# Identity matmuls while the first keys load, and the first four heads cast and split two by two

## The chip, the core and the metric

The kernel runs on one core of a Trainium2 chip. Its time is the device time of one execution in microseconds, taken as the median of several runs. The engines named below are PE (TensorE matmul) with PEld (its weight loads), DVE (VectorE), ACT (ScalarE), POOL (GpSimd) and SP (SyncE), which here only issues transfers. Each engine works through its own instructions in order, and semaphores hold an instruction back until the work it needs is done.

## What is computed

Sliding-window attention with sink keys (2 batches, 8 heads, 768 positions, head dimension 64) feeds a capacity-limited expert layer, and that feeds a gated layer:

```python
scores = q @ k.T / 8, kept where key < n_sink or 0 <= row - key < window
x = softmax(scores) @ v                      # (1536, 512)
logits = x @ w_gate                          # each token gets one of 8 experts, 192 tokens each
out[mask_e] = relu(x[mask_e] @ w1[e]) @ w2[e]
return ((out @ w_a) * (out @ w_b)) @ w_out
```

## The kernel before

The program has three stages. The attention works on 12 blocks of 128 rows (2 batches, 6 each); then comes the choice of experts; then the expert and gated layers, all in one instruction stream per engine that is written in the order in which it runs.

A block's keys and queries come as one tile `kq` (`load`, line L220), two transfers per block, one for each half of the 128 partitions. For blocks 0 and 1 each of the two is cut again, so that heads 0 to 3 and heads 4 to 7 arrive separately: four transfers of 256 KB per block. All of them stand in SP's queue, in order, and a transfer has to wait for the one that stands eight transfers ahead to have landed, because eight semaphores serve them in turn.

`split_half` prepares four heads of block 0 or 1: ACT casts the keys into `KH` (L243) and the queries into `q` (L244), DVE writes the rest of the keys into `KL` (L245) and the rest of the queries into the lower half of `q` (L246). Later blocks are split by `split` on DVE (L256, L258) and POOL (L257, L259).

`run` then goes through groups of four heads, 24 in all. `scores` does for each head two matmuls into the PSUM tile `sp` (L282, L283), a masked copy with its minimum on DVE (L284), and the exponential on ACT (L286). `turn` transposes with the identity (L300), `values` multiplies by V (L326), `rows` transposes back and multiplies by the gate weights into the PSUM tile `x` (L341). ACT's order in the first round is: casts of heads 0 to 3, two exponentials, casts of heads 4 to 7.

The PSUM pool gives each tile name a fixed number of buffers. `x` has one buffer. Each call of `pp.tile(..., name="x", bufs=1)` makes a new tile on that buffer, which may be written only when the work on the tile before is over. The identity `ident` is made on POOL at the very start. Before the change the first matmul of the program is that of the first scores.

Of the kernel before, what the change touches and what calls it, by code (L numbers as in the profile page):

```python
# [8 lines left out]
F32 = mybir.dt.float32  # L9
# [10 lines left out]
B, H, S, D = 2, 8, 768, 64  # L20
# [12 lines left out]
KC = [0, 128, 256, 416, 544, 704]  # L33
# [18 lines left out]
def kq_start(b, j):  # L52

    return (b * KTOT + KC[j] + 128 * (NJ * b + j)) * D * H


def dram_ap(src, offset, ap):
    return bass.AP(tensor=src.tensor, offset=src.offset + offset, ap=ap)
# [83 lines left out]
class Attention:  # L142
# [70 lines left out]
    def load(self, i):  # L213
        nc, at = self.nc, self.at
        b, j = self.blocks[i]
        w = KW[j]
        r = self.raws[i] = at.tile([128, H, 288], F32, name="kq", bufs=3)
        for h0, h1 in ((0, 4), (4, H)) if i < 2 else ((0, H),):
            for half in range(2):
                nc.sync.dma_start(r[64 * half:64 * half + 64, h0:h1, :w + 128],  # L220
                                  dram_ap(self.kq, kq_start(b, j) + h0 * (w + 128),
                                          [[H * (w + 128), 64], [w + 128, h1 - h0], [1, w + 128]]))
# [10 lines left out]
                nc.sync.dma_start(v[32 * r:32 * r + 32, :, r // 2, 64 * (r % 2):64 * (r % 2) + 64],  # L233
                                  dram_ap(self.vS, (b * 128 + 32 * r) * 2 * D, [[2 * D, 32], [D, 2], [1, D]]))

    def split_half(self, i, half, copy, eng):

        nc = self.nc
        if half == 0:
            self.Q[i] = self.at.tile([128, H, 128], F32R, name="q", bufs=3)  # L240
        hs, c = slice(4 * half, 4 * half + 4), KC[i]
        r, q, kh, kl = (t[:, hs] for t in (self.raws[i], self.Q[i], self.KH[:, :, c:c + 128], self.KL[:, :, c:c + 128]))
        copy(kh, r[:, :, :128])  # L243
        copy(q, r[:, :, 128:256])  # L244
        eng.tensor_tensor(kl, r[:, :, :128], kh.bitcast(F32), op=OP.subtract)  # L245
        return lambda: nc.vector.tensor_tensor(q[64:], r[64:, :, 128:256], q[64:].bitcast(F32), op=OP.subtract)  # L246
# [14 lines left out]
    def run(self, extra):  # L261

        nc, at, pp, ident = self.nc, self.at, self.pp, self.ident
# [7 lines left out]
        def scores(g):  # L271
            i, q = divmod(g, 2)
            b, j = blocks[i]
            c0, w, co, cp, cs = kwin(j)
            if q == 0:
                MN[i] = at.tile([128, H], F32, name="mn", bufs=3)
                SM[i] = at.tile([128, H], F32, name="sm", bufs=4)
            p = P[g] = at.tile([128, 4, 288], F32, name="p", bufs=3)
            out = []
            for h in range(4 * q, 4 * q + 4):  # L280
                sp = pp.tile([128, 288], F32, name="sp", bufs=3)
                nc.tensor.matmul(sp[:, :w], Q[i][:, h], KH[:, h, c0:c0 + w], start=True, stop=False)  # L282
                nc.tensor.matmul(sp[:, :w], Q[i][:, h], KL[:, h, c0:c0 + w], start=False, stop=True)  # L283
                nc.vector.tensor_tensor_reduce(p[:, h % 4, :w], sp[:, :w], self.mask(j), -0.125, 1e30, op0=OP.add,  # L284
                                               op1=OP.min, accum_out=MN[i][:, h:h + 1])
                out.append(lambda h=h: nc.scalar.activation(p[:, h % 4, :w], p[:, h % 4, :w], AF.Exp, bias=MN[i][:, h:h + 1],  # L286
                                                            scale=-1.0, accum_out=SM[i][:, h:h + 1]))
            return out

        def turn(g):  # L290
            i, q = divmod(g, 2)
            c0, w, co, cp, cs = kwin(blocks[i][1])
            p = P[g]
            nsl = 2 if cp is None else 4
            out = []
            for e in range(2):
                tp = pp.tile([128, 4, 128], F32, name="tp", bufs=2)
                for t in range(nsl):
                    c = co if t < 2 else cp
                    nc.tensor.transpose(tp[:, t], p[:, 2 * e + t % 2, c:c + 128], ident)  # L300
                t = T[g, e] = at.tile([128, 4, 128], F32, name="t", bufs=5)
                out.append(lambda t=t, tp=tp: nc.scalar.activation(t[:, :nsl], tp[:, :nsl], AF.Copy))
            return out

        def turn_sink(g):
            i, q = divmod(g, 2)
            cs = kwin(blocks[i][1])[4]
            if cs is not None:
                sp = pp.tile([128, 128], F32, name="ts", bufs=1)
                for h in range(4):  # L310
                    nc.tensor.matmul(sp[NS * h:NS * h + NS], P[g][:, h, cs:cs + NS], ident, start=True, stop=True, skip_group_check=True)
                ST[g] = at.tile([128, 128], F32, name="st", bufs=3)
                nc.vector.tensor_copy(ST[g], sp)
# [20 lines left out]
        def rows(g):  # L334

            i, q = divmod(g, 2)
            x = X[g] = (pp.tile([128, 288], F32, name="sp", bufs=3).rearrange("p (a n) -> p a n", a=2) if g == ng - 1
                        else pp.tile([128, 2, 144], F32, name="x", bufs=1))
            os = OS.pop(g)
            for a in range(2):  # L340
                nc.tensor.matmul(x[:, a], os[:, a], self.ig[:, 2 * q + a].rearrange("p c d -> p (c d)"), start=True, stop=True)  # L341

        def out_rows(g):
            i, q = divmod(g, 2)
            x = X.pop(g)
            hs = slice(4 * q, 4 * q + 4)
            if q == 0:
                XR[i] = self.pre.tile([128, H, D + E], F32, name="xr", bufs=2)
                r = RS[i] = self.pre.tile([128, 2, H], F32, name="rs", bufs=2)
                nc.scalar.activation(r[:, 0], SM[i], AF.Identity, bias=tiny)  # L350
                nc.vector.reciprocal(r[:, 1], r[:, 0])
            nc.vector.tensor_tensor(XR[i][:, hs], x.rearrange("p a (c d) -> p (a c) d", c=2),
                                    RS[i][:, 1, hs][:, :, None].to_broadcast([128, 4, D + E]), op=OP.mult)
            if q == 1:
                nc.vector.tensor_reduce(self.L[:, i], XR[i][:, :, D:].rearrange("p h e -> p e h"), op=OP.add, axis=AX.X)
                nc.sync.dma_start(self.xd[128 * i:128 * i + 128].rearrange("p (h d) -> p h d", h=H), XR[i][:, :, :D])
# [1 line left out]
        self.load(1)  # L358
        self.load(2)
        self.load_v(0)  # L360
        self.split_half(0, 0, nc.scalar.copy, nc.vector)()
        for it in range(-1, ng + 2):
            if it % 2 and (it + 1) // 2 < nb:
                i = (it + 1) // 2
                if i + 1 < nb:
                    self.load_v(i + 1)
                if i + 3 < nb:
                    self.load(i + 3)
            exps = scores(it + 1) if it + 1 < ng else []
            if 0 <= it - 3:  # L370
                out_rows(it - 3)
            for e in exps[:2]:
                e()
            if it == -1:
                self.split_half(0, 1, nc.scalar.copy, nc.vector)()
            elif it == 0:
                self.second()
                for half in range(2):
                    self.split_half(1, half, nc.scalar.copy, nc.vector)()
            elif it == 1:  # L380
                self.others()
                self.split(2, nc.gpsimd)
            elif it % 2 == 0 and it // 2 + 2 < nb:
                self.split(it // 2 + 2, nc.gpsimd)
            ts = turn(it) if 0 <= it < ng else []
            for e in ts[:1]:
                e()
            for e in exps[2:]:
                e()
            for e in ts[1:]:  # L390
                e()
            if 0 <= it < ng:
                turn_sink(it)
            if 0 <= it - 1 < ng:
                copy = values(it - 1)
            if 0 <= it - 2 < ng:
                rows(it - 2)
            if 0 <= it - 1 < ng:
                copy()
            if it == 20:  # L400
                self.wide()
            if it in extra:
                extra[it]()
# [697 lines left out]
```

## Time and profile before

| | |
|---|---|
| median of 3 runs | 641.16 us (639.24 to 641.59) |
| profiled execution | 640.13 us, span 638.3 us |
| PE busy | 582.6 us, 91% of the span |
| DVE, ACT, POOL busy | 361.5, 250.4, 102.4 us |
| mean granted TensorE clock | 0.965 of full speed |
| attention / choice / experts | to about 127 us / to about 166 us / to the end |

The profiled execution is about 1.0 us below the median of the runs. The span is counted from the first to the last instruction and is what the rows below give times in; some 1.8 us lie around it. In the rows, a timeline line gives start, duration, engine, line of the kernel, operation, tiles and shapes, how many were merged (x), and in brackets how long the engine stood idle ahead of it and what ended that. A matmul of plain 32-bit floats appears as two records, each with a weight load of its own; the scores' matmuls and the transposes of L300 appear as one.

### The profile page before, as it was taken

The numbers are of one execution on the slowest core, as the hardware profiler recorded it, in microseconds if no ns is written. First come the engines' busy times: TensorE is split into PE (matmuls) and PEld (weight loads), VectorE is DVE, ScalarE is ACT, GpSimd is POOL, SyncE is SP. The second block draws the span as 40 slices with busy tenths as digits, with TensorE's granted clock in tenths as the row PEclk, the third lists the DMA queues.
The fourth block names the chain that finished last, engine by engine and source line by source line (L and its number), as shares of the span: only waits on it lengthen the run. The fifth ranks groups of instructions, "written<-read, shape, count | busy, mean of one in ns | idle before, by whom it ended". The sixth has DMA issues, their size and how long they took to land.

```text
span 638.3 us, 10373 instructions
## 1 busy us (share of the span) xinstructions
PE 582.6 (91%) x3804; PEld 542.7 (85%) x3804; DVE 361.5 (57%) x913; ACT 250.4 (39%) x655; POOL 102.4 (16%) x150
## 2 busy tenths in 40 slices
PE   3899989922699999999999999999999999999996
PEld 2688868711599999999999999999999999998885
DVE  5776786687336766666633655565557456622330
ACT  4677777600245554554422322322233222322330
POOL 2567765122401010000000000000000000012021
PEclk9999999955699999999999999999999999999998
DMA  9998594420477878767600222222222222102010
GB/s 181 224 205 180 113 265 150 132 83 2 124 235 225 252 233 273 251 197 264 216 16 0 67 67 68 98 67 70 92 71 75 79 79 66 34 17 82 2 67 33
DMA packets 49804, 79.04 MB, mean 124 GB/s; under 512 B 16944, under 2 KB 25168, under 8 KB 49232
## 3 DMA queue, kind: packets, MB, share of 16 engines
q1 hardware_dynamic: 47616, 71.97, 40.4%
q0 software_dynamic: 1984, 6.31, 3.3%
q8 instruction: 32, 0.52, 0.4%
q14 instruction: 28, 0.23, 0.1%
q10 hardware_dynamic: 144, 0.00, 0.0%
HBM read 71.98 MB, written 6.29 MB: 123 GB/s over the span
## 4 chain that ended last, share of the span: by engine, by line
PE 64%; issue 7%; POOL 1%; DVE 0%; ACT 0%; POOLq 0%
PE b L851 13%; PE b L906 10%; PE b L904 10%; PE b L905 10%; PE b L865 8%; PE b L866 4%; PE b L928 3%; PE b L927 3%; PE b L926 3%; POOL out L944 1%; PE b L841 1%; PE b L956 1%; DVE ys L875 0%; ACT y L877 0%; POOLq L1097 0%
## 5 line engine op out<-in xcount | busy, mean ns | idle before, releaser
L906 PE MATMUL b<-y,ml 128*128 128x384 f32 x384 | 128.6, 335 | 0.0
L904 PE MATMUL b<-y,mh 128*128 128x384 f32 x384 | 128.6, 335 | 0.0
L905 PE MATMUL b<-y,mh 128*128 128x384 f32 x384 | 128.5, 335 | 0.0
L851 PE MATMUL b<-xm,wr 128*128 128x192 f32 x512 | 89.1, 327 | 0.1
L851 PEld LDWEIGHTS b<-xm,wr 128*128 128x128 f32 x512 | 82.4, 190 | 0.3 <-issue 0.3
L865 PE MATMUL b<-hh,wh 128*128 128x384 f32 x256 | 79.5, 374 | 0.0
L904 PEld LDWEIGHTS b<-y,mh 128*128 128x128 f32 x384 | 72.1, 188 | 1.1
L905 PEld LDWEIGHTS b<-y,mh 128*128 128x128 f32 x384 | 72.1, 188 | 1.0
L906 PEld LDWEIGHTS b<-y,ml 128*128 128x128 f32 x384 | 72.1, 188 | 0.0
L761 DVE TENSOR_TENSOR wl<-wr,wh 128x512 fp32r<-128x512 f32 x60 | 41.5, 691 | 41.8 <-ACT wh L755 39.3
L944 POOL DMA_INDIRECT out<-xg,idx x6 | 6.2, 1040 | 361.9 <-ACT xg L942 361.1
L866 PE MATMUL b<-hh,wl 128*128 128x192 f32 x256 | 64.1, 250 | 0.0
L286 ACT ACTIVATE p<-p,mn 128x288 f32<-128x288 f32 (+2 forms) x96 | 47.8, 500 | 27.0 <-DVE mn L284 27.0
L282 PE MATMUL sp<-KH,q 128*128 128x288 f32 (+2 forms) x96 | 33.2, 360 | 18.2 <-DVE q L246 12.3
L866 PEld LDWEIGHTS b<-hh,wl 128*128 128x128 f32 x256 | 48.9, 191 | 0.0
L284 DVE CUSTOM_DVE_ANT_0 p<-sp,mk 128x288 f32<-128x288 f32 (+2 forms) x96 | 35.8, 420 | 22.2 <-PE sp L283 21.2
L865 PEld LDWEIGHTS b<-hh,wh 128*128 128x128 f32 x256 | 48.1, 188 | 0.0
L282 PEld LDWEIGHTS sp<-KH,q 128*128 128x128 f32 x96 | 20.1, 209 | 24.2 <-DVE q L246 12.9
L755 ACT ACTIVATE wh<-wr 128x512 fp32r<-128x512 f32 x64 | 39.9, 624 | 0.4 <-DMA wr<-in_w 0.4
L853 ACT ACTIVATE hh<-b 128x192 fp32r<-128x192 f32 x64 | 20.9, 327 | 46.2 <-PE b L851 45.4
L915 ACT ACTIVATE zz<-z 128x384 fp32r<-128x384 f32 x24 | 12.6, 525 | 58.8 <-DVE z L910 58.8
L257 POOL TENSOR_TENSOR KL<-kq,KH 128x1024 fp32r<-128x1024 f32 (+1 forms) x10 | 29.0, 2896 | 40.0 <-DVE KH L256 39.2
(245 smaller groups left out, 1038.3 us busy)
## 6 DMA issues: line engine op xcount, KB each, us to landing
wr<-in_w SPq DMA_DIRECT2D x128, 256.0 KB, 4.2
mr<-in_wm SPq DMA_DIRECT2D x36, 512.0 KB, 3.7
kq<-in_kq SPq DMA_DIRECT2D x12, 512.0 KB, 7.4
kq<-in_kq SPq DMA_DIRECT2D x8, 576.0 KB, 9.8
v<-in_vN SPq DMA_DIRECT2D x12, 256.0 KB, 8.6
xd<-xr SPq DMA_DIRECT2D x12, 256.0 KB, 4.4
kq<-in_kq SPq DMA_DIRECT2D x8, 256.0 KB, 5.3
xg<-xd,idx POOLq DMA_INDIRECT x12, 3.6
```

The costliest lines, as they stand in the source:

```text
L257: eng.tensor_tensor(kl, kr, kh.bitcast(F32), op=OP.subtract)
L282: nc.tensor.matmul(sp[:, :w], Q[i][:, h], KH[:, h, c0:c0 + w], start=True, stop=False)
L284: nc.vector.tensor_tensor_reduce(p[:, h % 4, :w], sp[:, :w], self.mask(j), -0.125, 1e30, op0=OP.add, op1=OP.min, accum_out=MN[i][:, h:h + 1])
L286: out.append(lambda h=h: nc.scalar.activation(p[:, h % 4, :w], p[:, h % 4, :w], AF.Exp, bias=MN[i][:, h:h + 1], scale=-1.0, accum_out=SM[i ...
L755: self.nc.scalar.activation(self.W[u][0], self.R[u, 1], AF.Copy)
L761: (eng or self.nc.vector).tensor_tensor(lo, self.R.pop((u, 1)), hi.bitcast(F32), op=OP.subtract)
L851: nc.tensor.matmul(ps, w[:, 128 * k:128 * k + 128], x[:, k], start=k == 0, stop=k == 3)
L865: nc.tensor.matmul(ps, hi[:, 128 * d:128 * d + 128], hh, start=f == 0, stop=False, skip_group_check=True)
L866: nc.tensor.matmul(ps[:, 0], lo[:, 128 * d:128 * d + 128], hh[:, 0], start=False, stop=f == 7, skip_group_check=True)
L904: nc.tensor.matmul(p, hi[:, w, c], y[:, k, 0], start=k == 0, stop=False)
L905: nc.tensor.matmul(p, hi[:, w, c], y[:, k, 1], start=False, stop=False)
L906: nc.tensor.matmul(p, lo[:, w, c], y[:, k, 0], start=False, stop=k == 3)
```

## The change

Two edits. Sixteen matmuls of the identity with itself go ahead of the first split, each into a newly made tile `x`. And the first four heads of block 0 come in transfers of two heads, and are cast and split two heads at a time; `split_half` becomes `split_some` with the heads given as a range, and does the same work for every later group.

```diff
-        for h0, h1 in ((0, 4), (4, H)) if i < 2 else ((0, H),):
+        for h0, h1 in ((0, 2), (2, 4), (4, H)) if i == 0 else ((0, 4), (4, H)) if i == 1 else ((0, H),):
             for half in range(2):
                 nc.sync.dma_start(r[64 * half:64 * half + 64, h0:h1, :w + 128],
...
-    def split_half(self, i, half, copy, eng):
+    def split_some(self, i, h0, h1, copy, eng):
...
-        hs, c = slice(4 * half, 4 * half + 4), KC[i]
+        hs, c = slice(h0, h1), KC[i]
...
-        self.split_half(0, 0, nc.scalar.copy, nc.vector)()
+
+        for k in range(16):
+            nc.tensor.matmul(pp.tile([128, 2, 144], F32, name="x", bufs=1)[:, 0, :128], ident, ident, start=True, stop=True)
+        self.split_some(0, 0, 2, nc.scalar.copy, nc.vector)()
+        self.split_some(0, 2, 4, nc.scalar.copy, nc.vector)()
...
-                self.split_half(0, 1, nc.scalar.copy, nc.vector)()
+                self.split_some(0, 4, 8, nc.scalar.copy, nc.vector)()
...
-                    self.split_half(1, half, nc.scalar.copy, nc.vector)()
+                    self.split_some(1, 4 * half, 4 * half + 4, nc.scalar.copy, nc.vector)()
```

How PE's instructions stand at the start of the program, with the semaphores each waits for. Before, the scores of the first group come first (`DVE_49` counts finished DVE work):

```order
L282 MATMUL sp<-KH,q 128x128 [waits DVE_49]
L283 MATMUL sp<-KL,q 128x128
L282 MATMUL sp<-KH,q 128x128
L283 MATMUL sp<-KL,q 128x128
L282 MATMUL sp<-KH,q 128x128
L283 MATMUL sp<-KL,q 128x128
```

And PE at the same place with the change (`Pool_49` counts POOL's work, here the identity; `PE_49` counts PE's own finished matmuls):

```order
L363 MATMUL x<-ident 128x128 [waits Pool_49]
L363 MATMUL x<-ident 128x128 [waits PE_49] x15
L282 MATMUL sp<-KH,q 128x128 [waits DVE_49]
L283 MATMUL sp<-KL,q 128x128
L282 MATMUL sp<-KH,q 128x128
L283 MATMUL sp<-KL,q 128x128
L282 MATMUL sp<-KH,q 128x128 [waits DVE_49]
L283 MATMUL sp<-KL,q 128x128
```

The sixteen stand ahead of every other matmul, and fifteen of them wait for PE's own count, which the one before each raises when it is done; the third head's scores now have a wait of their own.

ACT at the start of the program, as a difference (casts of block 0, exponentials of the first group, casts of heads 4 to 7):

```order
-L243 CAST KH<-kq 128x4x128
-L244 CAST q<-kq 128x512
+L243 CAST KH<-kq 128x2x128
+L244 CAST q<-kq 128x256
+L243 CAST KH<-kq 128x2x128
+L244 CAST q<-kq 128x256
 L286 ACTIVATE p,sm<-p,mn 128x128 x2
 L243 CAST KH<-kq 128x4x128
```

Two casts became four of half the size; the casts of heads 4 to 7 still stand behind the first two exponentials. DVE's L245 and L246 change in the same way. SP issues four transfers of 128 KB in place of the first two of 256 KB:

```order
-L220 DMA kq<-in_kq 64x4x256 x8
+L220 DMA kq<-in_kq 64x2x256 x4
+L220 DMA kq<-in_kq 64x4x256 x6
 L220 DMA kq<-in_kq 64x2304 x2
 L228 DMA v<-in_vN 128x512 x2
```

The bytes and their order by heads are the same; the queue is two transfers longer.

## Rows read from the trace of the kernel before

**Rows 1.** The page: span.

```profile
span 638.3 us, 10373 instructions
```

**Rows 2.** The chain that ended last, its earliest work.

```profile
166.37 3.75 PE b L956 x8
```

**Rows 3.** Stretches: busy us of PE, PEld, DVE, ACT, POOL; granted clock, DMA share, GB/s.

```profile
4.00:8.00 4.00, 0.00 (x0) 0.00 (x0) 2.54 (x10) 1.14 (x2) 1.43 (x4) 1.00 1.13 217
8.00:12.00 4.00, 1.97 (x8) 1.78 (x8) 2.58 (x11) 2.35 (x9) 0.00 (x0) 1.00 1.13 203
...
24.00:27.00 3.00, 3.00 (x18) 2.34 (x17) 0.94 (x3) 2.45 (x9) 2.92 (x2) 1.00 1.17 253
```

**Rows 4.** Timeline, the first 11 us.

```profile
1.04 0.29 POOL masks.py:199 TENSOR_SCALAR_AFFINE_SELECT ident<-ident 128x128 f32<-128x128 f32 x1
...
5.71 0.23 DVE L170 TENSOR_SCALAR mk<-mk 128x128 f32<-128x128 f32 x1
6.47 0.62 ACT L243 CAST KH<-kq 128x512 fp32r<-128x512 f32 x1 [4.22 <-DMA kq<-in_kq]
...
7.84 0.69 DVE L246 TENSOR_TENSOR q<-kq,q 64x512 fp32r<-64x512 f32 x1
8.59 0.29 PEld L282 LDWEIGHTS sp<-KH,q 128*128 128x128 f32 x1 [8.59 <-DVE q L246]
...
8.86 0.42 PE L283 MATMUL sp<-KL,q 128*128 128x128 f32 x1
...
9.07 0.41 PE L282 MATMUL sp<-KH,q 128*128 128x128 f32 x1
...
9.31 0.29 DVE L284 CUSTOM_DVE_ANT_0 p<-sp,mk 128x128 f32<-128x128 f32 x1 [0.78 <-PE sp L283]
...
10.48 0.60 ACT L243 CAST KH<-kq 128x512 fp32r<-128x512 f32 x1
```

**Rows 5.** Timeline: lone 32-bit matmuls at 157 and 126 us, and who reads them.

```profile
126.74 0.76 PE L341 MATMUL sp<-ig,os 128*128 128x144 f32 x4
127.53 0.46 DVE L352 TENSOR_TENSOR xr<-sp,rs 128x288 f32<-128x288 f32 x1 [0.19 <-PE sp L341]
...
157.56 0.50 PEld L576 LDWEIGHTS ps<-dc,on 128*128 128x128 f32 x2
...
158.19 0.17 DVE L581 TENSOR_SCALAR bad<-ps 128x8 f32<-128x8 f32 x1 [0.18 <-PE ps L576]
```

**Rows 6.** Timeline of PE: score matmuls at 22 and at 33 us.

```profile
22.25 0.41 PE L282 MATMUL sp<-KH,q 128*128 128x256 f32 x1
22.47 0.41 PE L283 MATMUL sp<-KL,q 128*128 128x256 f32 x1
...
33.28 0.29 PE L282 MATMUL sp<-KH,q 128*128 128x288 f32 x1
33.41 0.30 PE L283 MATMUL sp<-KL,q 128*128 128x288 f32 x1
```

**Rows 7.** Stretches during and after the eight matmuls of L956.

```profile
169.00:170.00 1.00, 1.00 (x4) 0.63 (x3) 0.67 (x1) 0.30 (x1) 0.00 (x0) 0.50 0.20 33
170.00:171.00 1.00, 1.00 (x9) 1.00 (x7) 0.64 (x1) 0.39 (x2) 0.00 (x0) 0.76 0.63 225
```

**Rows 8.** Tile kq: the second and third transfer (durations of issue, then times to landing).

```profile
L220 SPq DMA_DIRECT2D kq<-in_kq x2: 613/615/617, 1.6 to 2.2; - x2
...
DMA to landing us min/median/max: 4.8/5.1/5.3
```

**Rows 9.** Timeline, blocks 2 and 3 being split.

```profile
25.80 2.35 POOL L259 TENSOR_TENSOR q<-kq,q 64x1024 fp32r<-64x1024 f32 x1
26.49 2.20 DVE L256 CAST KH<-kq 128x1024 fp32r<-128x1024 f32 x1 [1.88 <-DMA kq<-in_kq]
28.20 0.40 PE L282 MATMUL sp<-KH,q 128*128 128x288 f32 x1 [0.48 <-POOL q L259]
...
29.55 0.44 DVE L284 CUSTOM_DVE_ANT_0 p<-sp,mk 128x288 f32<-128x288 f32 x1
```

More of the change, by code (lines that the diff above doesn't have):

```diff
@@ L234, in load_v @@
                                   dram_ap(self.vS, (b * 128 + 32 * r) * 2 * D, [[2 * D, 32], [D, 2], [1, D]]))
-    def split_half(self, i, half, copy, eng):
+    def split_some(self, i, h0, h1, copy, eng):
         nc = self.nc
-        if half == 0:
+        if h0 == 0:
             self.Q[i] = self.at.tile([128, H, 128], F32R, name="q", bufs=3)
-        hs, c = slice(4 * half, 4 * half + 4), KC[i]
+        hs, c = slice(h0, h1), KC[i]
         r, q, kh, kl = (t[:, hs] for t in (self.raws[i], self.Q[i], self.KH[:, :, c:c + 128], self.KL[:, :, c:c + 128]))
```

## The prediction

> **What bounds the kernel now.** The page first: the span is 638.3 us [rows 1], and 640.13 us are the profiled execution's time. The chain of waits comes next, but it reaches back only to 166.37 us, the eight matmuls ahead of the experts [rows 2]. The edits act in the first 15 us, so the question is whether a shift there comes out at the end. For that I read the stretches and then the timeline of the start. Up to 8 us PE has nothing to do [rows 3]: the first keys are on their way. The timeline shows the opening chain: ACT waits for the transfer until 6.47, casts, DVE ends the last subtraction at 7.84 + 0.69 = 8.53, PE begins the first scores at 8.59, DVE reads them at 9.31, and ACT, after two exponentials, casts heads 4 to 7 from 10.48 [rows 4]. Everything after hangs on that chain, since ACT and DVE work in order: the later casts stand behind these exponentials.
>
> Is there slack further on that would swallow a shift? The one transfer that DVE waits for later is block 3's, for 1.88 us, until 26.49. But the cast it starts takes 2.20 us, while POOL works on block 2 until 25.80 + 2.35 = 28.15; the next scores start at 28.20, on POOL's heels [rows 9]. So that wait hides behind the POOL chain, which began with the first scores. I take a shift at 9 us as one at the end, less at most the 29.55 - (28.20 + 0.5) = 0.85 us by which DVE's reading of those scores (some 0.5 us after PE's start) is late because of that cast.
>
> **The change part by part.** *Halved transfers.* The second transfer lands at 1.6 + 4.8 = 6.4 us, the third at 2.2 + 5.3 = 7.5 to 7.6 [rows 8], so 256 KB take about 1.2 us in the queue and the first lands at about 5.2 (estimate). Two transfers of 128 KB for heads 0 and 1 are the same 256 KB: about 5.2 instead of 6.4, and heads 2 and 3 at 6.4. Issuing takes SP about 0.6 us each [rows 8]; two more cost 1.2 us of SP, whose transfers queue for longer than that, so the later blocks' bytes do not come later. Price 0; if the small transfers starve the engines at the start, up to +0.6 us on heads 4 to 7, which are not needed before 10.48.
>
> *Halved casts and subtractions.* ACT's cast of 512 columns takes 0.62 us, DVE's subtraction 0.69 [rows 4]; halves cost between half and the whole of that, I take 0.4 each. DVE is busy with the mask until 5.71 + 0.23 = 5.94 [rows 4]. Heads 0 and 1: ACT from 5.25 on, DVE at about 5.95 to 6.75. Heads 2 and 3: ACT from 6.45, DVE about 6.9 to 7.7. So the first scores could begin at 6.8 instead of 8.59, and DVE, whose subtractions for heads 2 and 3 stand ahead of the first reading, could read at about 7.75 instead of 9.31: a gain of about 1.5 us, if PE were free.
>
> *Sixteen matmuls.* The identity is ready at 1.04 + 0.29 = 1.33 [rows 4], so PE starts at about 1.4. Each of the other fifteen waits until PE's count says that the one before it is done, which the order shows; so what counts is the whole time of a lone matmul, weight load to count, not the step of a stream. No row shows such a wait on the matmul just before. The nearest rows: the first score pair is two 128-column passes, each with its weight load, just as one identity matmul is two records; from the first load at 8.59 to the end of the second pass at 8.86 + 0.42 = 9.28 it takes 0.69 us, and DVE starts 0.03 later [rows 4]. A lone 32-bit matmul of 8 columns takes from 157.56 to DVE's 158.19, 0.63 us [rows 5], and 120 columns more in each of two passes can add up to 0.2. PE in turn starts 8.59 - 8.53 = 0.06 after DVE ended [rows 4]. So a step is 0.69 + 0.05 = 0.74 us, at most 0.85, at the slow clock. The bottom end is the fast clock: two matmuls of four records at 126.74 end 0.03 before DVE's 127.53, so 0.76 us for both; the second adds two passes of about 0.12, which leaves 0.5 for one and 0.55 with the wait.
>
> Which clock? The column of granted clock reads 1.00 from the start, but nothing ran on PE before 8.59, and the starts say otherwise: 256 columns 0.22 us apart at 22.25, 288 columns 0.13 apart at 33.28 [rows 6], that is the 1.2 and the 2.4 GHz level. Between lies a stretch in which PE was busy without a break (24 to 27) [rows 3]. At 166.37 eight matmuls stream back to back for 3.75 us [rows 2], and the granted clock goes from 0.50 to 1.00 just after them, in the microsecond from 170 [rows 7]. Scores with gaps between (1.97 us busy of 4 at 8 to 12) [rows 3] did not raise it, though those go on for 12 us. Sixteen matmuls that each wait for the last leave the array idle for much of each step (two loads and two passes of about 0.11 in 0.74), so they resemble the second case; I take the slow level throughout.
>
> Then the sixteen end at 1.4 + 16 x 0.74 = 13.2, and the first scores, whose operands have been ready since 6.8, start at about 13.1 instead of 8.59 (a load may begin a little ahead of the end before it). Queued behind them on PE are all scores; DVE's reading waits for these, ACT's exponentials for DVE, and the casts of heads 4 to 7 stand behind those. **Sum: +4.5 us** on the profiled execution, 640.13 + 4.5 = 644.6. That execution is 1.0 us under the median of the runs, 641.16, from which the same sum gives 645.7. I predict 645.2. The bounds: steps of 0.85 us end at 15.0, +6.4, thus 646.5 to 647.6; the 0.85 us of slack make the least 643.8.
>
> The Trainium skill, TensorE: Matmul & The Clock Gate, section Single matmul latency, gives (219 + N)/1.2 ns for one matmul at the slow clock, 289 ns for 128 columns. Taken for the whole step with one more pass it would be about 0.4 us by that page (an estimate), sixteen would end near 7.7 us, and nothing would be delayed. The rows say 0.69 for the two passes with their loads.
>
> **The rivals.** *A: the sixteen raise the clock.* For it: PE would be occupied from 1.4 on without a long gap. Against it: the gaps inside each step, and that later bursts of scores did not do it. If the level rose halfway, eight steps of 0.74 and eight of 0.55 end at 1.4 + 5.9 + 4.4 = 11.7, +3.1 on the first scores; had it been high from the start, 10.2, +1.6. The fast level then gives back, up to 27 us: a pair of score matmuls takes 0.43 at the slow level (8.86 less 0.21 to 9.07, twice [rows 4]) and half at the fast one, 0.6 us over three pairs of a group and 0.2 on the first pair's latency; 0.8 for each of about four groups, 3.2 at most, less where DVE or ACT is the slower. Net between -1.6 and +0.6: 639.5 to 641.8 on the median, middle 641. The same page's table at the end advises to warm up with matmuls ahead of the work that matters; by it this rival is the case, and only the waits between the matmuls speak against it.
>
> *B: the waits cost next to nothing, PE overlaps the matmuls.* This ends on the other side. The step would be that of the score stream, 0.21 us [rows 4], the sixteen end at 4.8, and the halved casts give their 1.5 us: 639.7 on the median, and 636.5 if the clock were up as well. It decides as soon as the step is below (6.8 - 1.4)/16 = 0.34 us. Against it stand the lone pair's 0.69 and the wait in the order.
>
> *C: the shift is swallowed*, by transfers that wait less or by DVE getting its casts of block 3 in earlier. For it: the 1.88 us wait [rows 9]. Against it: POOL's chain ends behind it. It would leave at most 4.5 - 1.9 = 2.6: 643.8.
>
> **How the numbers follow.** The forecast has 0.62, A 0.18, B 0.10, C 0.10. Half a per cent, about what a measurement of this kernel can tell from no change, is 3.2 us. In the forecast the time is above 644.4 in about 0.55 of the 0.62 (the rest is a step near 0.69 with some slack); A adds 0.01 above and 0.03 below 638, B 0.05 below, C 0.02 above. Faster 0.08, same 0.34, slower 0.58. The range from 639.0 to 648.0 takes in the forecast with its bounds, C and nearly all of A, and leaves out half of B and clocks that rise late; the likeliest case's own range is 643.5 to 647.8.
>
> **What would show it.** In the profile of the changed kernel: sixteen groups of two L363 records from about 1.4 us, 0.7 to 0.8 us apart (0.55 would be A, 0.21 B), PE's first L282 at about 13 with nothing but PE ahead of it, ACT's first cast at about 5.3, DVE's last subtraction of the four heads at about 7.7, then DVE idle until about 13.8 on L283. The casts of heads 4 to 7 come at about 15.0, and PE's start of block 2 at about 32.7 instead of 28.20. The start of the experts' matmuls at 166.37 moves to about 170.8; if it moves by clearly less than the first scores, something took up the shift that I did not see. The forecast is wrong if 256-column scores already step by 0.11 us before 20 us, or if the sixteen are over by 8 us.

## The result, and the profile after

The changed kernel takes 647.07 us (median of 6 runs, 646.05 to 648.13), the kernel before in the same comparison 641.12 us (6 runs, 639.24 to 641.59). The ratio is 1.0089, with a 95% interval of 1.0072 to 1.0107: slower by 0.9%, 5.95 us. (A ratio, here and below, is an estimate of its own beside the medians and need not be their quotient.) The profiled execution takes 646.05 us, 5.92 more than that of before.

The start of the timeline of the kernel after (columns as in [rows 4]; the lines of the code have moved by up to 4):

```profile
1.38 0.50 PEld L363 LDWEIGHTS x<-ident 128*128 128x128 f32 x2 [1.38 <-POOL ident masks.py:199]
1.38 13.60 PE L363 MATMUL x<-ident 128*128 128x128 f32 x32 [1.38 <-POOL ident masks.py:199]
...
2.23 0.50 PEld L363 LDWEIGHTS x<-ident 128*128 128x128 f32 x2 [0.35 <-PE x L363]
...
5.23 0.41 ACT L243 CAST KH<-kq 128x256 fp32r<-128x256 f32 x1 [2.98 <-DMA kq<-in_kq]
...
6.35 0.40 ACT L243 CAST KH<-kq 128x256 fp32r<-128x256 f32 x1 [0.42 <-DMA kq<-in_kq]
...
7.25 0.42 DVE L246 TENSOR_TENSOR q<-kq,q 64x256 fp32r<-64x256 f32 x1
...
14.18 0.50 PEld L363 LDWEIGHTS x<-ident 128*128 128x128 f32 x2 [0.35 <-PE x L363]
...
14.63 0.45 PE L282 MATMUL sp<-KH,q 128*128 128x128 f32 x1
...
14.88 0.42 PE L283 MATMUL sp<-KL,q 128*128 128x128 f32 x1
...
15.10 0.42 PE L282 MATMUL sp<-KH,q 128*128 128x128 f32 x1
...
15.34 0.29 DVE L284 CUSTOM_DVE_ANT_0 p<-sp,mk 128x128 f32<-128x128 f32 x1 [7.67 <-PE sp L283]
...
16.50 0.60 ACT L243 CAST KH<-kq 128x512 fp32r<-128x512 f32 x1
```

The sixteen take one merged PE row, so their rhythm is read from PEld: a pair of loads every 0.853 us (14.18 less 1.38, over fifteen steps), each time after 0.35 us idle that a matmul of the same line ends. The operands are ready at 7.25 + 0.42 = 7.67, and DVE then stands idle for 7.67 us. The first scores come at 14.63, 6.04 later than in [rows 4], DVE's first reading 6.03 later, the casts of heads 4 to 7 6.02 later (10.48 before). The wait is invisible in PE's busy time. The stretches of the kernel after:

```profile
4.00:8.00 4.00, 3.77 (x10) 2.45 (x10) 3.30 (x12) 1.42 (x4) 1.44 (x4) 1.00 0.96 207
8.00:12.00 4.00, 3.71 (x11) 2.38 (x10) 0.00 (x0) 0.00 (x0) 0.00 (x0) 1.00 1.14 227
```

PE reads as 93% busy where it does nothing that anyone needs, while DVE, ACT and POOL have nothing at all to do from 8 to 12. The same timeline around blocks 2 and 3, which answers to [rows 9], and the chain, which answers to [rows 2]:

```profile
28.05 0.42 PE L283 MATMUL sp<-KL,q 128*128 128x256 f32 x1
...
28.27 0.42 PE L282 MATMUL sp<-KH,q 128*128 128x256 f32 x1
...
28.45 3.28 POOL L257 TENSOR_TENSOR KL<-kq,KH 128x1280 fp32r<-128x1280 f32 x1 [23.02 <-DVE KH L256]
...
30.55 1.73 DVE L256 CAST KH<-kq 128x1024 fp32r<-128x1024 f32 x1
...
31.81 2.68 POOL L259 TENSOR_TENSOR q<-kq,q 64x1024 fp32r<-64x1024 f32 x1
...
34.55 0.40 PE L282 MATMUL sp<-KH,q 128*128 128x288 f32 x1 [0.86 <-POOL q L259]
...
34.79 0.29 PE L283 MATMUL sp<-KL,q 128*128 128x288 f32 x1
34.92 0.30 PE L282 MATMUL sp<-KH,q 128*128 128x288 f32 x1
...
35.30 0.44 DVE L284 CUSTOM_DVE_ANT_0 p<-sp,mk 128x288 f32<-128x288 f32 x1
```

```profile
172.38 3.75 PE b L960 x8
```

DVE's cast of block 3 no longer waits for its transfer. Block 2's first scores are 6.35 us later, their reading 5.75, the experts' matmuls 6.01: what was lost at 15 us is lost at the end. Score matmuls right behind the sixteen step by 0.22 us (14.88 to 15.10), 256 columns still by 0.22 at 28, and 288 columns by 0.13 at 34.8, as in [rows 6]: the sixteen raised no clock.

One more row is worse than before. The transfers issued at 4.2 and 4.9 us (tile kq; the first of them ends heads 4 to 7):

```profile
L220 SPq DMA_DIRECT2D kq<-in_kq x2: 616/616/616, 4.2 to 4.9; - x2
...
DMA to landing us min/median/max: 6.4/6.4/6.4
```

4.2 + 6.4 = 10.6 us for heads 4 to 7. In the kernel before their last transfer was issued at 2.9 and took 5.9 us, 8.8 us:

```profile
L220 SPq DMA_DIRECT2D kq<-in_kq x1: 616/616/616, 2.9 to 2.9; - x1
...
DMA to landing us min/median/max: 5.9/5.9/5.9
```

In the changed kernel nobody needs them until 16.50.

### The profile page after: what moved, and what is told of

Same layout as the page of the kernel before. It is cut to its first block, busy times and chain, and to the rows that moved or that the text cites. A ratio compares the mean times of both kernels' runs of the same rounds, so it can differ in the third digit from the quotient of the medians.

```text
span 644.3 us, 10445 instructions
## 1 busy us (share of the span) xinstructions
PE 595.0 (92%) x3836; PEld 550.7 (85%) x3836; DVE 363.8 (56%) x915; ACT 250.9 (39%) x657; POOL 102.9 (16%) x150
## 4 chain that ended last, share of the span: by engine, by line
PE 63%; issue 7%; POOL 1%; DVE 0%; ACT 0%; POOLq 0%
PE b L855 13%; PE b L908 10%; PE b L910 10%; PE b L909 10%; PE b L869 8%; PE b L870 3%; PE b L932 3%; PE b L931 3%; PE b L930 3%; POOL out L948 1%; PE b L845 1%; PE b L960 1%; DVE ys L879 0%; ACT y L881 0%; POOLq L1101 0%
```

## The experiments

Times in us. "Before" is the median of the kernel before on the same chip in the same comparison. The last four columns are places in each profiled execution: the first score matmul, DVE's first reading, ACT's cast of heads 4 to 7, DVE's first reading of block 2. The profiled execution lies 1.3 to 4.4 us above the median in *twenty-four*, *fillers*, *stream and casts*, *halves only* and *one tile*, and within 1.1 us of it in the others.

| kernel | median (range, runs) | before | ratio [95%] | scores | read | cast 4-7 | block 2 |
|---|---|---|---|---|---|---|---|
| before | 641.12 (639.24-641.59, 6) | | | 8.59 | 9.31 | 10.48 | 29.55 |
| after | 647.07 (646.05-648.13, 6) | 641.12 | 1.0089 [1.0072, 1.0107] | 14.63 | 15.34 | 16.50 | 35.30 |
| halves only | 641.06 (639.74-645.87, 12) | 641.24 | 0.9996 [0.9978, 1.0014] | 6.79 | 7.68 | 10.38 | 31.63 |
| one tile | 641.99 (638.96-646.40, 12) | 641.24 | 1.0015 [0.9990, 1.0040] | 7.62 | 8.08 | 10.40 | 32.05 |
| sixteen only | 646.79 (646.13-648.93, 6) | 641.24 | 1.0094 [1.0076, 1.0112] | 14.64 | 15.34 | 16.50 | 35.31 |
| six | 640.74 (638.86-644.15, 12) | 641.24 | 0.9997 [0.9979, 1.0015] | 6.79 | 7.67 | 9.54 | 28.65 |
| casts only | 640.34 (639.50-642.33, 12) | 641.85 | 0.9982 [0.9966, 0.9998] | 7.87 | 8.76 | 9.88 | 28.96 |
| transfers only | 640.45 (639.76-646.49, 12) | 641.85 | 0.9990 [0.9968, 1.0011] | 8.15 | 8.88 | 10.04 | 29.31 |
| stream and casts | 640.01 (639.15-642.14, 12) | 641.85 | 0.9967 [0.9951, 0.9982] | 7.84 | 8.73 | 9.85 | 28.94 |
| twenty-four | 653.72 (652.88-655.04, 5) | 641.85 | 1.0182 [1.0153, 1.0211] | 21.46 | 22.16 | 23.33 | 42.15 |
| late gate | 641.19 (638.51-643.98, 12) | 641.42 | 0.9998 [0.9981, 1.0014] | 6.48 | 7.37 | 8.63 | 30.36 |
| score pairs | 646.82 (646.24-647.30, 4) | 641.42 | 1.0084 [1.0061, 1.0108] | 14.18 | 14.85 | 16.01 | 34.82 |
| fillers | 640.39 (639.49-642.04, 12) | 641.07 | 0.9990 [0.9976, 1.0004] | 7.92 | 8.81 | 9.93 | 29.53 |
| block 3 first | 640.12 (639.24-642.36, 12) | 641.80 | 0.9983 [0.9966, 1.0000] | 7.93 | 8.82 | 9.94 | 28.86 |

### Which half of the change costs the time

*Halves only*: the change without the sixteen.

```diff
-        for k in range(16):
-            nc.tensor.matmul(pp.tile([128, 2, 144], F32, name="x", bufs=1)[:, 0, :128], ident, ident, ...)
```

> The sixteen matmuls are left out; the halved transfers, casts and subtractions stay. Theory W (the sixteen wait for one another and hold PE until 15 us; that is the whole loss): the 6 us are gone. How much below the kernel before it lies tells the price of the halves. W as predicted: the first DVE reading of scores moves from 9.31 to about 7.7, time 639.5. Theory L (the halved transfers land later: the second transfer of heads 4 to 7 landed at 4.2 + 6.4 = 10.6 us in the changed kernel, at 2.9 + 5.9 = 8.8 before): ACT's cast of heads 4 to 7 waits for it until about 10.6, against 10.48 before, and the gain of 1.5 us is lost again, time 641 to 641.5. Theory H (the halves cause the loss): 647.

*Sixteen only*: the sixteen ahead of transfers and casts as they were before.

```diff
-        for h0, h1 in ((0, 2), (2, 4), (4, H)) if i == 0 else ((0, 4), (4, H)) if i == 1 else ((0, H),):
+        for h0, h1 in ((0, 4), (4, H)) if i < 2 else ((0, H),):
...
-        self.split_some(0, 0, 2, nc.scalar.copy, nc.vector)()
-        self.split_some(0, 2, 4, nc.scalar.copy, nc.vector)()
+        self.split_some(0, 0, 4, nc.scalar.copy, nc.vector)()
```

> The sixteen waiting matmuls without the halves (transfers, casts and subtractions of four heads at a time as before). W: PE is held until 15 us, both ways of splitting are done by then, so the time is that of the changed kernel, 647 within 0.5 us. Theory H: 641. A price of the halves that PE's delay does not hide would show as a time below 646.5.

The sixteen alone give 646.79 and the places of the changed kernel to 0.01 us: they are the whole loss. The halves alone give no measurable gain, though DVE's first reading comes 1.63 us earlier. The timeline of the kernel with the halves only, ACT and then DVE, shows where that goes:

```profile
10.38 0.62 ACT L243 CAST KH<-kq 128x512 fp32r<-128x512 f32 x1 [1.49 <-DMA kq<-in_kq]
```

```profile
30.09 0.69 DVE L256 CAST KH<-kq 128x1024 fp32r<-128x1024 f32 x1 [4.52 <-DMA kq<-in_kq]
31.63 0.45 DVE L284 CUSTOM_DVE_ANT_0 p<-sp,mk 128x288 f32<-128x288 f32 x1
```

ACT is done with its first exponentials at 8.9, but heads 4 to 7 have not landed until 10.38: the gain is gone by the second group. Block 3 lands 3.6 us later than in [rows 9], and in this execution block 2 is read 2.1 us later than before. Another 1.6 us go just behind it: the next group is read 3.7 us late, and the granted clock is 0.57 there, where the kernel before has 1.00. The kernel with the halves only, then the kernel before:

```profile
32.00:36.00 4.00, 3.86 (x26) 3.44 (x26) 1.88 (x10) 3.26 (x10) 3.92 (x2) 0.57 1.03 189
37.16 0.46 DVE L284 CUSTOM_DVE_ANT_0 p<-sp,mk 128x288 f32<-128x288 f32 x1 [3.24 <-PE sp L283]
```

```profile
33.48 0.46 DVE L284 CUSTOM_DVE_ANT_0 p<-sp,mk 128x288 f32<-128x288 f32 x1 [1.74 <-PE sp L283]
```

### Is it the waits between the sixteen, and their number?

*One tile*: the sixteen write one tile made once, so none of them waits.

```diff
+        warm = pp.tile([128, 2, 144], F32, name="x", bufs=1)
         for k in range(16):
-            nc.tensor.matmul(pp.tile([128, 2, 144], F32, name="x", bufs=1)[:, 0, :128], ident, ident, ...)
+            nc.tensor.matmul(warm[:, 0, :128], ident, ident, ...)
```

> As the changed kernel, but the sixteen matmuls write one tile that is made once, so that none waits for the one before; same arithmetic, same count, halves kept. W: they step by 0.2 to 0.43 us, end between 4.8 and 8.3 us, the first scores start at about 6.8 or with their end, time within 0.5 us of the kernel without the sixteen, 639.5 to 641.5. Rival S (the sixteen cost PE's time whether they wait or not): 13.6 us as before, time 647. Rival A (without gaps they raise the clock): score matmuls of 128 columns step by 0.11 instead of 0.21 us in the first 20 us, time 636 to 638.

Its timeline and its stretches:

```profile
1.39 6.48 PE L364 MATMUL x<-ident 128*128 128x128 f32 x32 [1.39 <-POOL ident masks.py:199]
...
7.77 0.28 PE L283 MATMUL sp<-KL,q 128*128 128x128 f32 x1
7.88 0.27 PE L282 MATMUL sp<-KH,q 128*128 128x128 f32 x1
```

```profile
8.00:12.00 4.00, 0.87 (x7) 0.64 (x6) 1.96 (x10) 2.48 (x9) 0.00 (x0) 0.80 1.12 216
12.00:16.00 4.00, 2.85 (x12) 2.44 (x12) 2.80 (x14) 2.74 (x9) 0.00 (x0) 0.50 1.11 231
```

Without the waits a step is 6.48 / 16 = 0.405 us on average, less than half. The first scores come 0.83 us later than with the halves only (7.62 against 6.79), but that costs nothing that the medians can tell. The execution shown is the slowest of the twelve (646.40): it loses its time behind the first scores, where DVE's cast of block 3 waits until 30.50. Score matmuls then step by 0.11 us, the 2.4 GHz level, but the granted clock reads 0.80 and then 0.50 in the next stretches: PE was busy for 0.87 us of the four in which it fell, waiting for heads 4 to 7.

*Six* and *twenty-four*: the change with another count, waits and all.

```diff
-        for k in range(16):
+        for k in range(6):
```

> As the changed kernel with six waiting matmuls in place of sixteen. W: 0.85 us each, they end at 1.4 + 6 x 0.85 = 6.5 us, before the operands of the first scores are ready at 6.8, so the time is that of the kernel without any, within 0.3 us. If each matmul costs the kernel its step wherever it stands, 5.1 us more than without any. Score matmuls still step by 0.21 us (slow clock).

> The change with twenty-four identity matmuls in place of sixteen, each waiting for the one before it. Theory S (the loss is the number of matmuls times a step of 0.853 us, less what lies ahead of the operands, and goes through to the end): eight more cost 8 x 0.853 = 6.8 us, 647.1 + 6.8 = 653.9, first scores at 21.45. Theory C (a longer delay is swallowed in part by transfers that are then in place): under 652. If the matmuls raised the clock in time, under 650.

The timelines of the two, six first:

```profile
1.38 5.06 PE L363 MATMUL x<-ident 128*128 128x128 f32 x12 [1.38 <-POOL ident masks.py:199]
6.79 0.47 PE L282 MATMUL sp<-KH,q 128*128 128x128 f32 x1 [0.34 <-DVE q L246]
```

```profile
1.38 20.43 PE L363 MATMUL x<-ident 128*128 128x128 f32 x48 [1.38 <-POOL ident masks.py:199]
21.46 0.45 PE L282 MATMUL sp<-KH,q 128*128 128x128 f32 x1
```

Six end before the operands come and cost nothing. Eight more than sixteen, expected at 8 x 0.853 = 6.82 us, put the first scores 6.83 and block 2 6.85 later; the medians differ by 6.65, and by 5.92 if each is taken against its own kernel before, which the intervals of the two ratios do not tell from 6.8. So the loss is the count times the step, less what lies ahead of the operands.

### Why the step is 0.853 and not 0.74

*Score pairs*: each of the sixteen made of the two passes by which the prediction sized them.

```diff
+        idr = self.at.tile([128, 128], F32R, name="idr")
+        nc.scalar.copy(idr, ident)
         for k in range(16):
-            nc.tensor.matmul(pp.tile([128, 2, 144], F32, name="x", bufs=1)[:, 0, :128], ident, ident, ...)
+            warm = pp.tile([128, 2, 144], F32, name="x", bufs=1)[:, 0, :128]
+            nc.tensor.matmul(warm, idr, idr, start=True, stop=False)
+            nc.tensor.matmul(warm, idr, idr, start=False, stop=True)
```

> The change with each of the sixteen made of the very two passes that the prediction sized them by: a rounded copy of the identity (one more copy on ACT, done by about 2.6 us) times itself twice into each newly made tile, as a head's two score matmuls are. Only the kind of the passes and the start differ from the change. Theory P (the step was mis-sized because a plain 32-bit matmul's first pass is longer than a score pass): step 0.69 + 0.05 = 0.74 us, sixteen from 2.65 end at 14.5, first scores at 14.4, 646.5. Theory W (the wait from one matmul's count to the next load is dearer than the 0.05 us that DVE's handover showed): step 0.85 again, end at 16.3, first scores at 16.0, 648.4.

Its timeline:

```profile
2.50 0.47 PE L366 MATMUL x<-idr 128*128 128x128 f32 x1 [2.50 <-ACT idr L363]
2.77 0.41 PE L367 MATMUL x<-idr 128*128 128x128 f32 x1
...
3.99 0.47 PE L366 MATMUL x<-idr 128*128 128x128 f32 x1
```

The step is 0.745 us (3.99 less 2.50 is two steps), and 646.82 us came out where 646.5 was expected. Theory P holds: the reckoning of a lone pair and of the wait was right to 0.01 us, but for score passes. A matmul of plain 32-bit floats takes 0.11 us more in each lone step, and that was not in the pair I took it from.

### Where the halves' gain goes, and whether it can be had

*Casts only* and *transfers only* part the halves; both leave the sixteen out. The first has `for h0, h1 in ((0, 4), (4, H)) if i < 2 else ((0, H),)` and two calls of `split_some`, the second the changed transfers and one call for heads 0 to 3.

> The halved casts and subtractions of heads 0 to 3 alone: transfers as before, no identity matmuls. ACT still waits until about 6.45 us for the 256 KB transfers; by the halves (0.31 and 0.42 us in the changed kernel) DVE ends heads 0 and 1 at about 7.6, heads 2 and 3 at about 8.45, first scores at 7.65 instead of 8.59, DVE reads at about 8.5 instead of 9.31, casts of heads 4 to 7 at about 9.65 instead of 10.48. Theory L (the halved transfers are what makes later transfers land late, and ate the 1.5 us in the kernel with both halves): here nothing lands late, so the 0.8 us go through to the end, 640.4 us against 641.2, and block 3 lands at about 26.8 as before. Theory M (the 1.5 us are swallowed anyway further on, whatever the transfers do): 641.2. The two are near each other, so the scatter and the places in the trace count as much as the median.

> The halved transfers alone: four transfers of 128 KB for heads 0 to 3, whole casts of four heads, no identity matmuls. The whole cast needs all four, so ACT starts at about 6.3 to 6.45 and the first scores stay at 8.5 or so. Theory L: heads 4 to 7 land at 10.3 to 10.6 instead of 8.8, now 0.1 us or less after the cast's own turn at 10.4, and block 3 lands 2 to 3 us late in most executions; 641.2 to 642.5, with a scatter of some 5 us. Theory M: as before, 641.2, with the scatter of before.

The halved casts alone gain 0.55 us at DVE's first reading and 0.59 at block 2, and their ratio lies just below 1. The halved transfers alone bring the first cast forward (6.03 against 6.47), but block 3 lands late again (DVE waits until 27.77), and nothing is gained that can be measured. Across all runs the five kernels with halved transfers and no long delay behind them spread over 5.3 to 7.4 us, the four with whole transfers over 2.6 to 3.1, at 12 runs each; the kernel before, with whole transfers, spreads over 3.3 to 4.7 at 17 to 29 runs. DVE's cast of block 3 starts at 27.0 to 30.5 in the halved ones and at 26.5 to 28.0 in the whole ones and the kernel before, in one execution each. So theory L, that it is the halved transfers that land late, is borne out by the spread and, with some overlap, by the places; the medians alone would not tell it from M.

A part of the lateness is one of issuing. SP's queue is two transfers longer, and block 3's second transfer is issued at 21.0 us with the halves only against 19.4 before; it then takes 8.9 us to land instead of 7.0. In *six*, halved too, the two are 19.6 and 7.3, so it varies.

*Late gate*: the halves without the sixteen, and the gate weights' two small transfers moved from POOL's queue to SP's, behind V's.

```diff
-            nc.gpsimd.dma_start(ig[64 * i:64 * i + 64, :, i, D:], ...)
...
         self.load_v(0)
+        for i in range(2):
+            nc.sync.dma_start(self.ig[64 * i:64 * i + 64, :, i, D:], ...)
```

> Halved transfers and halved casts, no identity matmuls, and POOL's two transfers of the gate weights (rows of 32 bytes, issued from 3.35 us on POOL's own queue) moved behind V's on SP's queue. Theory I (those small rows, which the halved transfers let in among block 0's, are what sets some of the 16 engines back and makes heads 4 to 7 land 1.8 us late): here the engines end together, heads 4 to 7 have landed by 8.8 to 9.0, their casts start at about 9.5, block 3 lands at about 26.8, and the 1.5 us go through: 639.5 to 640 against 641.2. Theory N (the halved transfers do it by themselves): heads 4 to 7 land after 9.5 again, block 3 after 27.5, and the time is that of the halves alone, 641, with a scatter of 5 us.

ACT and DVE in its timeline (the line numbers are lower by three):

```profile
8.63 0.62 ACT L240 CAST KH<-kq 128x512 fp32r<-128x512 f32 x1
```

```profile
28.82 0.69 DVE L253 CAST KH<-kq 128x1024 fp32r<-128x1024 f32 x1 [4.49 <-DMA kq<-in_kq]
```

Neither theory came out whole. Heads 4 to 7 are now cast from 8.63, the first group is read at 7.37 and the second at 11.48, 1.8 us earlier than before: as far as one execution of each tells, the small rows were what held up heads 4 to 7. But DVE waits for block 3 until 28.82, block 2 is read 0.8 us later than before, and the median is that of before. Block 3's second transfer is issued at 21.4 us and takes 7.4: most of its lateness against 19.4 and 7.0 is one of issuing, in a queue that this edit itself made two transfers longer still. So the run does not part the two theories for block 3, and what makes the time to landing grow in *halves only* is left open.

*Stream and casts*: the casts only, and fifteen identity matmuls into one tile, timed to end ahead of the operands.

> Fifteen identity matmuls into one tile, without waits between them, transfers as before, halved casts. The fifteen end at about 1.4 + 15 x 0.405 = 7.5 us, just ahead of the first operands (7.6), so they cost nothing. If a stream that fills PE raises the clock and the rise is kept while the scores come close behind, 2 to 3 us come back: 638 to 639. If the clock falls again as soon as the scores leave gaps, as it did in the kernel with one tile and halved transfers (up at 7, down at 10.4 us), the time is that of the kernel with the halved casts alone, 640.4.

This is the fastest version, 640.01 us, ratio 0.9967 [0.9951, 0.9982]; its interval overlaps that of the casts only, and its places up to block 2 are the same to 0.03 us, so what the stream adds to the casts is not shown. Its profiled execution (642.14, the slowest of the twelve) loses 2.8 us behind block 2, where the next group is read at 35.68 against 32.89 with the casts only, and the granted clock is low in that stretch:

```profile
28.00:32.00 4.00, 3.21 (x17) 2.63 (x18) 3.18 (x13) 1.91 (x6) 3.71 (x2) 0.60 0.95 203
32.00:36.00 4.00, 4.00 (x26) 3.64 (x26) 0.32 (x1) 1.72 (x6) 1.34 (x1) 0.55 1.10 208
35.68 0.46 DVE L284 CUSTOM_DVE_ANT_0 p<-sp,mk 128x288 f32<-128x288 f32 x1 [4.28 <-PE sp L283]
```

With the casts only it reads 1.00 in both stretches.

*Fillers*: the stream and casts, and three more lots of streaming matmuls in PE's waits.

```diff
+            if it == -1:
+                for k in range(10):
+                    nc.tensor.matmul(warm[:, 0, :128], ident, ident, start=True, stop=True)
...
+            if it == 0:
+                for k in range(8):
+                    nc.tensor.matmul(warm[:, 0, :128], ident, ident, start=True, stop=True)
+            if it == 2:
+                warm = pp.tile([128, 128], F32, name="ts", bufs=1)
+                for k in range(10):
+                    nc.tensor.matmul(warm, ident, ident, start=True, stop=True)
```

> The fifteen streaming identity matmuls with the halved casts and the transfers of before, and three more lots of them put where PE waits in the first 28 us: ten behind the first group's scores, eight behind the second group's transposes, ten ahead of block 2's scores (into the PSUM tile that holds the sinks' scores later). Rival A's price: with the fast level from about 5 us on, score matmuls step by 0.11 instead of 0.21 us through the first four groups and up to 3.2 us come back by the prediction's reckoning; the rise there was bought with 13 us of waiting, here it costs nothing if each lot ends in its gap (10 x 0.2 = 2.0 us in a gap of 2.4). Then 637.5 to 639. If DVE and ACT, not PE, set the pace of these groups, the level brings nothing over the kernel without the three lots: 640. If the level falls in spite of them, the lots take twice as long, run past their gaps by 1.6 us each, and the time is 641 to 644.

PE and DVE in its timeline:

```profile
9.44 2.45 PE L379 MATMUL x<-ident 128*128 128x128 f32 x20
...
12.20 0.27 PE L283 MATMUL sp<-KL,q 128*128 128x128 f32 x1
12.31 0.27 PE L282 MATMUL sp<-KH,q 128*128 128x128 f32 x1
```

```profile
27.99 0.70 DVE L256 CAST KH<-kq 128x1024 fp32r<-128x1024 f32 x1 [4.89 <-DMA kq<-in_kq]
29.53 0.45 DVE L284 CUSTOM_DVE_ANT_0 p<-sp,mk 128x288 f32<-128x288 f32 x1
```

The fast level held from the first group on (steps of 0.11 us at 12.2) and DVE's reading of group 2 came forward from 18.54 to 17.30. Of these 1.24 us 0.60 are the halved casts' (17.94 with the casts only), so the level is worth 0.64 there. None of it arrives in this execution: DVE then waits 4.89 us for block 3 and reads block 2 at 29.53, where the kernel before read it at 29.55. None of the three cases in the expectation had this end: the level is worth something, if far less than 3.2 us, and the transfer takes it.

*Block 3 first*: the fillers, with block 3 loaded ahead of block 1's V.

```diff
+                if i == 0:
+                    self.load(3)
                 if i + 1 < nb:
                     self.load_v(i + 1)
-                if i + 3 < nb:
+                if 0 < i and i + 3 < nb:
                     self.load(i + 3)
```

> The kernel with the fillers, and block 3's keys and queries loaded ahead of block 1's V and sinks' V instead of behind them. In the kernel with the fillers DVE read the scores 1.5 us earlier than before in group 3 (22.67 against 24.18) and no earlier at all in block 2 (30.28 against 30.30), since its cast of block 3 waited until 27.99 for the transfer. Theory F (what is gained in the first 24 us stops at block 3's transfer, the losses pass): block 3 now lands by about 24, DVE does not wait for it, block 2 is read at about 28.8, and 1 to 2 us come out at the end: 639.2 to 640 against 641.2. Theory G (the gain is lost at POOL's chain or at another transfer, V's for instance, that is now late): 641 or more, with the first wait in the trace at that place.

SP and DVE in its timeline:

```profile
12.01 1.23 SPq L220 DMA_DIRECT2D kq<-in_kq  x2
```

```profile
26.97 0.69 DVE L256 CAST KH<-kq 128x1024 fp32r<-128x1024 f32 x1 [3.63 <-DMA kq<-in_kq]
...
28.86 0.46 DVE L284 CUSTOM_DVE_ANT_0 p<-sp,mk 128x288 f32<-128x288 f32 x1 [0.27 <-PE sp L283]
```

The two transfers are issued 5 us earlier than with the fillers alone (17.04) and land only 1.0 us earlier. Block 2 is read 0.67 us earlier, so the place is right, and 0.9983 [0.9966, 1.0000] is the time of the casts only. The condition of theory F, block 3 landed by 24, was not met; what a block 3 in time would be worth stays untried.

## Why the prediction was right, and where it was off

**The direction and the place** were right: a chain of sixteen, fifteen of which wait on PE's own count, with the operands ready from 6.8 us on and the halved casts worth nothing behind PE. *One tile* shows that the waits, not the matmuls, are the cost, *sixteen only* that they are all of it.

**The step** was mis-sized: 16 x 0.74 in the sum, 16 x 0.853 measured. The difference of 1.8 us is all that separates 13.2 from the 14.98 at which the sixteen end. The first scores come only 1.5 us later than forecast (14.63 against 13.1), since they start 0.35 us ahead of that end and not 0.1. The sum of +4.5 is short by the same 1.4 or 1.5 us (644.6 against 646.05 in the profiled execution, 645.7 against 647.07 in the median); the other 0.5 us to the forecast of 645.2 is that it was set between the two. The value lay at the upper bound of 0.85, which came from the lone 32-bit matmul of [rows 5], the same kind of instruction; I chose the score pair, which is another kind. *Score pairs* measured my row at 0.745.

**The halved casts** went as worked out: ACT from 5.23 (5.25), DVE done at 7.67 (7.7).

**The halved transfers** at price 0, at most +0.6 us on heads 4 to 7, were wrong: those heads landed at 10.6 instead of 8.8. The sentence that they are not needed before 10.48 holds for the kernel before; with the earlier scores they are wanted at 8.9. In the change the sixteen cover it. Without them it takes the whole 1.5 us that the halves were reckoned to give. Nor are the transfers behind them as early as before, which the prediction had reckoned with: V's first is issued at 9.21 in the changed kernel and at 8.93 with the halves only, against 7.61 before.

**The slack** of up to 0.85 us was not used: +6.04 at the first scores, +6.01 at the experts.

**Rival A** (the clock rises) falls for this kernel: steps of 0.22 us at 28 us. Its reckoning of what a raised clock gives back, up to 3.2 us, was far too high: with the fillers, fast from the first group on, DVE's first reading of group 2 is 0.64 us and the last of group 3 0.92 us ahead of the casts only (17.30 against 17.94, 22.67 against 23.59). Even this is cut off at block 3's transfer. The Trainium skill, TensorE: Matmul & The Clock Gate, section Why this matters for your kernels, has matmuls ahead of a measurement as the way to warm up. The traces agree that a stream without waits raises the level (0.11 us steps in *one tile*), and no run here shows a gain from it. **Rival B** (waits cost nothing) needed a step below 0.34 us; even without waits it is 0.405 on average. **Rival C** (the shift is swallowed) falls with the 6.01.

Behind all of this stands an asymmetry that the prediction saw only in part. A delay at the start passed whole: the changed kernel has 6.0 us at the first reading and at the experts, and *sixteen only* and *score pairs* have 5.6 and 6.1 at the experts. A gain passes only as far as block 3's transfer: in no kernel here did DVE's cast of block 3 start before 26.4 us. With the halves only it started at 30.09, with the fillers at 27.99, and there the gain was gone. Where it started by 27.0 (*casts only*, *stream and casts*, *six*, *block 3 first*), block 2 was still read 0.6 to 0.9 us early. That so small a gain reaches the end is hardly shown by the ratios, and a fall of the clock behind block 2 can take it, as in *stream and casts*.

## What to carry to other kernels

Filler matmuls must be free of each other: a tile made anew on a single buffer for each of them turns them into a chain of full latencies, and only what ends before the real operands are ready is free. Size such a chain from a row of the same kind of instruction, since two passes of another type can be 0.11 us apart. Before speeding up a start, look for the transfer that ends last in it; cutting earlier transfers smaller can make that one later (here by more than 1 us in four of five kernels, one execution each).

## What the runs showed of the hardware

- The column of granted clock reads 1.00 in the kernels before and after from the first stretch on, while matmuls there step at the slow level (0.22 us for 256 columns at 22 and at 28 us). The steps of like matmuls are the surer reading.
- DVE's cast of block 3 (1024 columns) takes 0.69 us when POOL is idle (*halves only*, 30.09) and up to 2.20 beside POOL's subtraction, and then it ends a fixed time after POOL does: 28.69 against 28.15 in [rows 9], 32.28 against 28.45 + 3.28 = 31.73 in the kernel after. That is 0.54 and 0.55 us, whenever the cast began; in the six other traces where the two meet it is 0.54 to 0.56. The Trainium skill, SBUF — State Buffer, section SBUF: two separate sides, has it that a DVE instruction that uses the port pair it shares with POOL and a POOL one block each other for the whole instruction. The rows agree if the cast is such an instruction, which no run here shows by itself.
- Two transfers of gate weights with rows of 32 bytes, next to four of 128 KB, went with heads 4 to 7 being cast from 10.38 (*halves only*) instead of 8.63 (*late gate*).
- Behind block 2 the granted clock was low in the traces of *halves only*, *one tile*, *stream and casts*, *score pairs* and *twenty-four* (0.50 to 0.86 in stretches of 4 us, 1.00 there in the other kernels), and in these five the next group came another 1.2 to 2.8 us late. How busy PE was just before does not tell which: from 24 to 28 us PE was busy for 1.80 us in *stream and casts*, where the clock then fell, and for 1.81 in *six*, where it did not.
